# Rounding of the weights by integer steps on three engines, with half of the feature turns moved ahead of the key sums

## The chip, the cores and the metric

The kernel runs on 1 core of one Trainium2 chip. The metric is the device time of one launch in microseconds (us), as the median of 3 runs. All engines of the core work at once: TensorE (PE, matmuls, transposes by matmul; PEld is its weight load), VectorE (DVE), ScalarE (ACT), GpSimd (POOL) and SyncE (SP, which here only issues DMAs). A queue of instructions belongs to each; an engine works its queue in order and waits on semaphores.

## The reference

```python
# polysketch attention, (batch, heads, seq, head_dim) = (4, 4, 1088, 32), r = 8
def phi(x):
    a = np.einsum('rd,bhsd->bhsr', S1, x)
    b = np.einsum('rd,bhsd->bhsr', S2, x)
    return np.einsum('bhsi,bhsj->bhsij', a, b).reshape(*x.shape[:-1], r * r)
q_p, k_p = (phi(q), phi(k))
kv = np.einsum('bhsf,bhsd->bhfd', k_p, v)
z = np.sum(k_p, axis=2)
num = np.einsum('bhsf,bhfd->bhsd', q_p, kv)
den = np.einsum('bhsf,bhf->bhs', q_p, z)[..., None] + 1e-06
attn = (num / den).astype(np.float32)
# bridge to (4352, 128), then a feed-forward block with d_ff = 2048
x = attn.transpose(0, 2, 1, 3).reshape(B * S, H * D)
h = x @ w_in
g = np.where(h > 0.0, h, np.exp(np.minimum(h, 0.0)) - 1.0)
out = (g @ w_out).astype(np.float32)
```

q, k and v are float32. S1, S2, w_in (128 x 2048) and w_out (2048 x 128) come as float64, so the kernel reads each weight as two 32-bit words, a low and a high one, and makes the float32 itself ("rounding" below).

## The kernel before

The schedule is written out by hand: the order of the Python calls is the order in each engine's queue.

**Groups and steps.** The 4352 rows of x are cut into 9 groups g of up to 512 rows, transposed (`xg`, 128 features by 512 rows). The 16 blocks of 128 hidden columns go in 8 pairs cp. A step (g, cp) is `mm1` (two matmuls of xg with W[:, cp], each in column strips by `quarters`, L256, into PSUM tiles h), then `elu`: on ScalarE a relu of -h (L861) and exp (L863) into e, on VectorE max(e - 1, h) into gg (L869); then, two steps later, the second product of that step: `mm2` (L256, o<-gg), `mm2_blocks` (L766) for group 1, or `mm2_seven` (L790) for later groups, which uses a 7-product scheme whose sums `sums7` GpSimd makes (L751 to L754) and whose weight sums SS `weights7` makes on GpSimd (L738). The loop over n at L1108 does mm1 of step n, then the extra work put there with `at`, then elu of the first half, the extra work of `mid`, elu of the second half, the extra work of `late`, then the second product of step n - 2. There are four h banks, so two steps.

**Start of the kernel.** Up to 16 us nothing of the feed-forward block can run: the key features (`KF`, `KO_first`), the key sums (`KA`, L435, into kv), their transpose (`KS_first`, L481 to L483: ScalarE copies kv to kd, TensorE transposes it, ScalarE copies the result to kvS), the query features qp (`q2_den`, `q2_out`, L588 to L609, in two halves), the turn of qp by TensorE transposes (`q4_early`, L621, two halves, each copied to qpT by ScalarE, L622), the product with kvS (`q5_early`, L628, xps) and the copies to xg (L634). `keep_warm` (L264) issues matmuls on constants into a bank nobody reads. The first two steps are written out by hand between L957 and L1000 (`mm1_first`, `elu_a`, `elu_d`), and the sums `KT_out(0)` (L444, a VectorE transpose of kv, with DMAs behind it) come at the end of step 3. kv lies in the PSUM bank ("o1") that `mm2_blocks` takes for group 1.

**The weights.** 16 loads of 256 KB (L174, on SP) fill raw tiles with the two words of each weight; five such tiles, which also serve as tt in `sums7`. Rounding goes in pieces (`order`, L177): pieces 0 to 5 are 256 columns wide (0: w_in of pair 0, 1: w_in of pair 1, 2 and 3: w_out of pairs 0 and 1, 4 and 5: w_in and w_out of pair 2), pieces 6 to 10 are both halves of pairs 3 to 7, 512 columns. One piece takes these passes:

- RA: `round_a` (L102, VectorE): W = high word AND the exponent's mask.
- RB: `round_b` (L107, ScalarE): relu(8 W + bias), the new exponent.
- RC: on VectorE `round_s` (L117, the sign), `round_m` (L121, the mantissa's high bits), `round_d` (L129, low word times 2^-32 plus those) and `round_e` (L137, product of both). For piece 7 the last is two GpSimd passes instead (L134, L135).

For pieces 0 and 1, sign, mantissa and `round_d` are done for both at once (`RC_2`). In the loop, RA stands in `at` of a step, RB in `late` of it, RC in `at` of the next; piece 6 has its RA at step 3, 5 at 4, 7 at 5, 8 at 7, 9 at 9, 10 at 11. In the start, q2_den(0) carries RA(0) between its parts and q2_out carries RA(1) between its halves.

**Other work that stands in the loop** and shares the queues: `transp` (L280, VectorE transposes of k and q), `KF_late_out` (L375), `KO` for batch 1 (L322, GpSimd, 1280 columns), `Z_share` and `make_SWs` (L316, L470, L471, GpSimd), and at step 12 the queries' sums (`queries`, L551 on TensorE; `q1_out_two`, L564, four VectorE transposes, two in `at`, two in `mid`).

Of the kernel before, what the change touches and what calls it, by code (L numbers as in the profile page):

```python
# [17 lines left out]
EXP = mybir.ActivationFunctionType.Exp  # L18
RELU = mybir.ActivationFunctionType.Relu
# [8 lines left out]
def kernel(  # L28
# [21 lines left out]
    nc = tc.nc  # L50
# [44 lines left out]
    tiny = const.tile([P, 1], F32, name="tiny")  # L95
    nc.gpsimd.memset(tiny[:], 2.0 ** -20)

# [14 lines left out]
    def words(raw):  # L112
        return (raw[:, :, 0], raw[:, :, 1]) if len(raw.shape) == 3 else (raw[:, :, :, 0], raw[:, :, :, 1])
# [17 lines left out]
    def round_e(raw, dst, pool=False):  # L131
        mant = words(raw)[0].bitcast(F32)
        if pool:
            nc.gpsimd.tensor_mul(mant, mant, _ap(tiny[:], [[0, dst.shape[1]]]))  # L134
            nc.gpsimd.tensor_mul(dst, mant, dst)  # L135
        else:
            nc.vector.scalar_tensor_tensor(dst, mant, 2.0 ** -20, dst, op0=MUL, op1=MUL)  # L137


    S16 = const.tile([2 * R, D], F32, name="S16")  # L140
# [38 lines left out]
    def round_w(f, i, *a):  # L179
        if wide:  # L180
            cp, w_in, w_out = order[i]
            c = slice(0 if w_in else 2 * P, 4 * P if w_out else 2 * P)
            f(raw_w[cp][:, c], W[:, cp, c], *a)

    def RA(i):
        round_w(round_a, i)

    def RB(i):
        round_w(round_b, i)


    def RC_2():
        if wide:
            for f in (round_s, round_m, round_d):
                f(raw_2[:, :, :2 * P], W[:, :2, :2 * P])

    def RS(i):
        round_w(round_s, i)

    def RM(i):  # L200
        round_w(round_m, i)

    def RD(i):
        round_w(round_d, i)

    def RE(i):
        round_w(round_e, i)

    def RC(i, pool=False):
        round_w(round_c, i)  # L210
        round_w(round_d, i)
        round_w(round_e, i, pool)

    load_v(0)
    load_w(0, 0)
# [260 lines left out]
            z_tile(0, ps, i)  # L476
        return ps, ZC(0, ps)

    def KS_first():
        kd = work.tile([P, 2, R * R], F32, name="kd", tag="kd", bufs=1)  # L480
        nc.scalar.copy(kd[:], _ap(kv_ps[0][:, :R * R], [[0, 2], [1, R * R]]))  # L481
        nc.tensor.transpose(kv_ps[0][:, 128:256], kd[:].rearrange("p w f -> p (w f)"), ident[:])
        nc.scalar.copy(kvS[:].rearrange("p h d -> p (h d)"), kv_ps[0][:, 128:256])  # L483

    NH = B * NT
# [35 lines left out]
    def q1_second():  # L521
        p = psum.tile([P, 512], F32, name="abwp", tag="h", bufs=4)
        for i in range(4):
# [5 lines left out]
        abw[1] = work.tile([P, H * 4, 3 * R], F32, name="abw1", tag="abq1", bufs=1)  # L529
        nc.scalar.copy(abw[1][:].rearrange("p (h t) y -> p h t y", h=H),  # L530
                       p[:, :384].rearrange("p (t h y) -> p h t y", t=4, h=H))
# [80 lines left out]
    def q4_early(g):  # L612

        qpT[g] = work.tile([P, H, 2, P], F32, name="qpT", tag="qpT", bufs=2)
        for hh in range(2):
            p = psum.tile([P, 512], F32, name="qtp", tag="aux")
            for h2 in range(2):
                for m in range(2):
                    o = (h2 * 2 + m) * P
                    r = (2 * hh + h2) * 4 + 2 * m  # L620
                    nc.tensor.transpose(p[:, o:o + P], qp[g][:, r:r + 2].rearrange("p t i j -> p (t i j)"), ident[:])  # L621
            nc.scalar.copy(qpT[g][:, 2 * hh:2 * hh + 2], p[:].rearrange("p (h m s) -> p h m s", h=2, m=2))  # L622

    def q5_early(g):
        xp = [psum.tile([P, 512], F32, name="xps", tag="aux") for _ in range(2)]
        for h in range(H):
            for w in range(2):
                nc.tensor.matmul(xp[w][D * h:D * h + D, :256], kvS[64 * w:64 * w + 64, h, :],  # L628
                                 qpT[g][64 * w:64 * w + 64, h].rearrange("p m s -> p (m s)"),
                                 skip_group_check=True, tile_position=(64 * w, D * h))  # L630
        xg[g] = work.tile([P, 512], F32, name="xg", tag="xg", bufs=3)
        to = xg[g][:].rearrange("p (m w s) -> p w m s", w=2, s=P)
        for w in range(2):
            nc.scalar.copy(to[:, w], xp[w][:, :256].rearrange("p (m s) -> p m s", s=P))  # L634


    exch = [raw_2[:, c].bitcast(F32).rearrange("p (e m a) w -> p e m (a w)", e=2, a=16) if wide else
# [319 lines left out]
    KO_first(7, KT)  # L957
    keep_warm(1, 96, 64)
    zq = q1z_first()
    q2_den(0, zq, lambda: RA(0))  # L960
    q2_out(0, 2, lambda: RA(1))
    KA(0)
    KS_first()
    keep_warm(1)
    RB(0)
    RB(1)
    q4_early(0)
    transp(qT, "q", 0, 8, NT)
    RC_2()
    RE(0)  # L970
    RE(1)
    q1_second()
    q5_early(0)
    keep_warm(1, 192, width[0])
    mm1_first()
    q2(1, 2, lambda: RA(2))
    RB(2)
    elu_a(0, 0, 0)
    elu_a(0, 0, 1, (0,))
    mm1(0, 1, (0,))  # L980
    q4_early(1)
    elu_d(0, 0, 0)
    mm1(0, 1, (1,))
    elu_a(0, 0, 1, (1,))
    RC(2)
    RA(3)
    elu_a(0, 1, 0, (0,))
    RB(3)
    q5_early(1)
    elu_d(0, 0, 1)  # L990
    mm2(0, 0, True, False)
    RA(4)
    for f in (RS, RM, RD):
        f(3)
    elu_a(0, 1, 0, (1,))
    elu_a(0, 1, 1)
    RB(4)
    elu_d(0, 1, 0)
    RE(3)
    elu_d(0, 1, 1)  # L1000


# [8 lines left out]
    def at(n, f, *a):  # L1011
        extra.setdefault(n, []).append((f, *a))
# [4 lines left out]
    def late(n, f, *a):  # L1017
        extra.setdefault((n, 1), []).append((f, *a))

    at(2, RC, 4)  # L1020
    for n, i in ((4, 6), (5, 5), (6, 7), (8, 8), (10, 9), (12, 10)):
        at(n - 1, RA, i)
        late(n - 1, RB, i)
        at(n, RC, i, i == 7)

    late(2, make_Sxp)
    late(3, keep_last, 0)
# [176 lines left out]
```

## Time and profile before

| what | value |
|---|---|
| timed runs | 262.29, 261.77, 261.96 us; median 261.96 |
| the profiled execution | span 260.6 us from the first to the last instruction; no other time is recorded for it; the median lies 1.36 us above the span |
| TensorE clock granted | 0.998 of full speed |
| busy before 16.25 us | PE 14.15, DVE 12.48, ACT 6.69, POOL 7.53 us |
| busy 16.25 to 30.30 (14.05 us) | PE 14.05, DVE 13.11, ACT 12.70, POOL 0 us |
| busy 30.30 to 63.00 (32.70 us) | PE 32.70, DVE 31.83, ACT 23.84, POOL 6.64 us |
| busy 63 to 257 (194 us) | PE 193.87, DVE 129.52, ACT 139.94, POOL 144.78 us |

Lines of the profile are read so: in a list of groups, "L102 DVE TENSOR_SCALAR W<-raw 128x256 uint32<-128x256 uint32 x6 | 1.7, 286 | 0.0" is line 102, its engine and operation, the tile written and the one read, the shapes, the count, total busy us, mean ns of one, and idle us before them. In a timeline or in the chain, the first two numbers are the start and the length in us; in brackets stands the idle time before and what ended it. A span can be of several instructions (x2). Consecutive passes of VectorE overlap by some 0.08 us where they do not depend on each other, those of ScalarE by some 0.10.

### The profile page before, as it was taken

The numbers are of one execution on the slowest core, as the hardware profiler recorded it, in microseconds if no ns is written. First come the engines' busy times: TensorE is split into PE (matmuls) and PEld (weight loads), VectorE is DVE, ScalarE is ACT, GpSimd is POOL, SyncE is SP. The second block draws the span as 40 slices with busy tenths as digits, with TensorE's granted clock in tenths as the row PEclk, the third lists the DMA queues.
The fourth block names the chain that finished last, engine by engine and source line by source line (L and its number), as shares of the span: only waits on it lengthen the run. The fifth ranks groups of instructions, "written<-read, shape, count | busy, mean of one in ns | idle before, by whom it ended". The sixth has DMA issues, their size and how long they took to land.

```text
span 260.6 us, 9756 instructions
## 1 busy us (share of the span) xinstructions
PE 254.8 (98%) x4123; PEld 158.4 (61%) x4123; DVE 186.9 (72%) x352; ACT 183.4 (70%) x358; POOL 159.0 (61%) x202
## 2 busy tenths in 40 slices
PE   8899999999999999999999999999999999999994
PEld 6753333453346667666666666665666666668993
DVE  6799999999988967997477675744466746544651
ACT  2379968766667577776687777775877777777792
POOL 3520007002179996788678798888688888887310
PEclk9999999999999999999999999999999999999999
DMA  5998079012112210002100204220001110110021
GB/s 173 330 358 222 3 223 268 24 21 85 28 18 28 31 34 18 3 15 34 20 0 4 33 10 104 60 30 13 3 3 27 34 26 3 25 19 3 3 30 33
DMA packets 30379, 15.61 MB, mean 60 GB/s; under 512 B 22496, under 2 KB 28000, under 8 KB 30336
## 3 DMA queue, kind: packets, MB, share of 16 engines
q1 hardware_dynamic: 29904, 14.63, 23.0%
q8 instruction: 32, 0.52, 0.9%
q10 hardware_dynamic: 368, 0.30, 0.3%
q0 software_dynamic: 64, 0.07, 0.1%
q14 instruction: 11, 0.09, 0.1%
HBM read 11.31 MB, written 2.36 MB: 52 GB/s over the span
## 4 chain that ended last, share of the span: by engine, by line
PE 97%; DVE 1%; ACT 0%; issue 0%; DVEq 0%
PE h L256 45%; PE pb L790 17%; PE pa L790 13%; PE o L256 5%; PE pb L766 4%; PE ol L256 3%; PE idle L264 1%; PE kv L435 1%; PE abp L343 1%; PE h L681 1%; PE h L551 1%; PE qtp L621 1%; DVE qp L609 1%; PE h L693 1%; PE xps L628 0%; PE kfps L365 0%
## 5 line engine op out<-in xcount | busy, mean ns | idle before, releaser
L256 PE MATMUL h<-xg,W 128*32 128x512 f32 (+3 forms) x904 | 130.8, 539 | 0.4 <-ACT xg L634 0.4
L869 DVE SCALAR_TENSOR_TENSOR gg<-e,h 128x512 f32<-128x512 f32 x128 | 85.9, 681 | 52.6 <-ACT e L863 47.8
L861 ACT ACTIVATE e<-h 128x512 f32<-128x512 f32 x128 | 75.5, 590 | 46.2 <-PE h L256 46.0
L863 ACT ACTIVATE e<-e 128x512 f32<-128x512 f32 x128 | 80.9, 632 | 3.8
L751 POOL TENSOR_TENSOR tt<-gg 128x512 f32<-128x512 f32 x50 | 64.3, 1286 | 28.9 <-DVE gg L869 25.2
L256 PEld LDWEIGHTS h<-xg,W 128*32 128x32 f32 (+1 forms) x904 | 43.0, 122 | 43.0 <-issue 34.4
L754 POOL TENSOR_TENSOR tt<-gg,tt 128x256 f32<-128x256 f32 x50 | 36.9, 739 | 3.9
L753 POOL TENSOR_TENSOR tt<-tt,gg 128x256 f32<-128x256 f32 x50 | 36.7, 734 | 3.9
L790 PEld LDWEIGHTS pa<-gg,W 128*64 128x64 f32 (+1 forms) x496 | 23.7, 126 | 22.4 <-issue 22.2
L790 PE MATMUL pa<-gg,W 128*64 128x128 f32 (+1 forms) x496 | 30.6, 274 | 0.0
L790 PE MATMUL pb<-tt,SS 128*64 128x128 f32 (+1 forms) x480 | 29.6, 273 | 0.0
L790 PEld LDWEIGHTS pb<-tt,SS 128*64 128x64 f32 (+1 forms) x480 | 22.8, 126 | 0.0
L790 PE MATMUL pa<-tt,SS 128*32 128x128 f32 (+1 forms) x288 | 21.2, 273 | 0.0
L790 PE MATMUL pb<-gg,SS 128*64 128x128 f32 (+1 forms) x256 | 19.9, 273 | 0.0
L790 PE MATMUL pb<-tt,W 128*64 128x128 f32 (+1 forms) x256 | 19.9, 273 | 0.0
L134 POOL TENSOR_TENSOR raw<-raw,tiny 128x512 f32<-128x512 f32 x1 | 1.0, 1041 | 24.7 <-DVE raw L129 24.7
L256 PE MATMUL o<-gg,W 128*32 128x512 f32 x128 | 15.3, 595 | 0.0
L790 PEld LDWEIGHTS pa<-tt,SS 128*32 128x32 f32 (+1 forms) x288 | 13.7, 124 | 0.0
L790 PEld LDWEIGHTS pb<-gg,SS 128*64 128x64 f32 (+1 forms) x256 | 12.8, 125 | 0.0
L790 PEld LDWEIGHTS pb<-tt,W 128*64 128x64 f32 (+1 forms) x256 | 12.8, 125 | 0.0
L766 PE MATMUL pb<-gg,W 128*32 128x256 f32 x192 | 11.5, 380 | 0.0
L921 DVE SCALAR_TENSOR_TENSOR gg<-e,h 128x256 f32<-128x256 f32 x16 | 6.6, 418 | 6.4 <-PE h L256 3.2
(163 smaller groups left out, 269.3 us busy)
## 6 DMA issues: line engine op xcount, KB each, us to landing
raw<-in_moe_w_in_dram SPq DMA_DIRECT2D x8, 256.0 KB, 6.3
raw<-in_moe_w_out_dram SPq DMA_DIRECT2D x8, 256.0 KB, 6.5
out_dram<-ob SPq DMA_DIRECT2D x112, 16.0 KB, 1.5
hd_k<-in_k_dram SPq DMA_DIRECT2D x3, 544.0 KB, 7.5
hd_q<-in_q_dram SPq DMA_DIRECT2D x3, 544.0 KB, 8.5
v<-in_v_dram SPq DMA_DIRECT2D x4, 288.0 KB, 7.1
v<-in_v_dram SPq DMA_DIRECT2D x4, 256.0 KB, 8.4
raw<-qpF SPq DMA_DIRECT2D x16, 64.0 KB, 2.0
```

The source lines that it names most:

```text
L256: nc.tensor.matmul(dst[c:c + tile], lhs[:, c:c + tile], rhs, skip_group_check=True, tile_position=(0, c), **kw)
L264: nc.tensor.matmul(idle[c:c + tile, :cols], ones[:, :tile], ones[:, :cols], skip_group_check=True, tile_position=(0, c))
L343: nc.tensor.matmul(ps[i // 5][64 * u:64 * u + 64, 64 * (i % 5):64 * (i % 5) + 64], kT[b][:, u * KT + i, :], Sab[:].rearrange("p h y -> p ( ...
L751: nc.gpsimd.tensor_tensor(_ap(t[:, 0], [[4 * P, 2], [P, 2], [1, P]]), _ap(gs[g, cp][:, 0, P:], [[4 * P, 2]] + us), _ap(gs[g, cp][:, 0], [[ ...
L753: nc.gpsimd.tensor_tensor(t[:, 1], t[:, 2], b11, op=ADD)
L754: nc.gpsimd.tensor_tensor(t[:, 3], b21, t[:, 1], op=SUB)
L766: nc.tensor.matmul(acc[1][0][r:r + width[0], 256 * hi:256 * hi + 256], lhs[:, w:w + width[0]], gg[:, c, 256 * u:256 * u + 256], start=(cp ...
L790: nc.tensor.matmul(bank[r:r + width[0], P * col:P * col + P], lhs[:, w:w + width[0]], rhs[:, u], start=(first and i in ((0,) if g == 1 els ...
L861: nc.scalar.activation(e, hs[g, cp][c][:, :n], RELU, scale=-1.0)
L863: nc.scalar.activation(e, e, EXP, scale=-1.0)
L869: nc.vector.scalar_tensor_tensor(gs[g, cp][:, c, :n], es[g, cp][:, c, :n], -1.0, hs[g, cp][c][:, :n], op0=ADD, op1=MAX)
L921: nc.vector.scalar_tensor_tensor(gs["last", k // 2][:, k % 2, :2 * P], es["last", k // 2][:, k % 2, :2 * P], -1.0, hs["last", k][:, :2 * P ...
```

## The change

Rounding now takes these passes for a piece, where lo and hi are the two words:

- strip: W = hi without the sign bit, on VectorE (an AND) or, for pieces 0 to 3, on ScalarE (Abs).
- floor: W = max(W, 2^-15) on VectorE; shift: W = W << 3 on VectorE.
- low: lo = 2^-51 lo + 2 on ScalarE (Identity), so that its bits are the rounded top bits of the low word.
- whole: W = W + lo as integers on GpSimd.
- `round_s`: the sign, on VectorE, as before.

So RA is strip, floor and shift; RB is low and whole; RC is `round_s` alone. `round_m` and `round_d` stay only for S1 and S2, `round_e` and `RC_2` are gone. In the loop RC moves from `at` to `mid`, behind the elu of the first half; `mid` entries stand in the order in which they are registered, so at step 12 it comes behind the first two `q1_out_two` transposes and ahead of the other two. The weight sums of the last two pairs move from `at` to `late` of step 12.

In the start, the first half of the turns of qp is issued on TensorE ahead of the transpose of the key sums, which was ahead of both; `KS_first` is cut into its ScalarE copy and the rest. VectorE copies half of the second qpT and one of the two xg halves of group 0. The second group's features (`q1_second`) are made in two parts, the second behind `q5_early`; the last `keep_warm` is 64 columns and not 192. On TensorE the order is now: key sums, keep_warm, four turns, the sums' transpose, four turns, half of q1_second, xps, the other half, keep_warm, the first h. In GpSimd's queue the whole passes of pieces 0 to 4 come ahead of make_Sxp and make_SWs, on ScalarE's strip(0), low(0) and strip(1) come ahead of kd, and low(1) between kvS and qpT.

```diff
+    def strip(raw, dst, eng=nc.vector):
+        if eng is nc.vector:
+            nc.vector.tensor_scalar(dst.bitcast(U32), words(raw)[1], 0x7FFFFFFF, None, op0=AND)
+        else:
+            nc.scalar.activation(dst, words(raw)[1].bitcast(F32), ABS)
+
+    def floor(raw, dst):
+        nc.vector.tensor_scalar_max(dst, dst, 2.0 ** -15)
+
+    def shift(raw, dst):
+        nc.vector.tensor_scalar(dst.bitcast(U32), dst.bitcast(U32), 3, None, op0=SHL)
+
+    def low(raw, dst):
+        lo = words(raw)[0]
+        nc.scalar.activation(lo.bitcast(F32), lo, IDENTITY, scale=2.0 ** -51, bias=two[:dst.shape[0]])
+
+    def whole(raw, dst):
+        nc.gpsimd.tensor_tensor(dst.bitcast(U32), dst.bitcast(U32), words(raw)[0], op=ADD)
...
     def RA(i):
-        round_w(round_a, i)
+        for f in (strip, floor, shift):
+            R1(f, i)
     def RB(i):
-        round_w(round_b, i)
+        R1(low, i)
+        R1(whole, i)
-    def RC(i, pool=False):
-        round_w(round_c, i)
-        round_w(round_d, i)
-        round_w(round_e, i, pool)
+    def RC(i):
+        R1(round_s, i)
...
+    def q4_out(g, hh, p, split=False):
+        if split:
+            nc.vector.tensor_copy(qpT[g][:, 2 * hh + 1], p[:, 2 * P:].rearrange("p (m s) -> p m s", m=2))
+            nc.scalar.copy(qpT[g][:, 2 * hh], p[:, :2 * P].rearrange("p (m s) -> p m s", m=2))
+        else:
             nc.scalar.copy(qpT[g][:, 2 * hh:2 * hh + 2], p[:].rearrange("p (h m s) -> p h m s", h=2, m=2))
...
         for w in range(2):
-            nc.scalar.copy(to[:, w], xp[w][:, :256].rearrange("p (m s) -> p m s", s=P))
+            (nc.vector.tensor_copy if split and w else nc.scalar.copy)(
+                to[:, w], xp[w][:, :256].rearrange("p (m s) -> p m s", s=P))
...
-    q2_den(0, zq, lambda: RA(0))
-    q2_out(0, 2, lambda: RA(1))
+    R1(strip, 0, nc.scalar)
+    R1(floor, 0)
+    R1(low, 0)
+    q2_den(0, zq)
+    q2_out(0, 2)
     KA(0)
-    KS_first()
     keep_warm(1)
-    RB(0)
-    RB(1)
-    q4_early(0)
+    R1(strip, 1, nc.scalar)
+    KS_first_a()
+    qpT_a = q4_early(0, (0,))
+    KS_first_b()
+    R1(low, 1)
+    R1(shift, 0)
+    R1(whole, 0)
     transp(qT, "q", 0, 8, NT)
-    RC_2()
-    RE(0)
-    RE(1)
-    q1_second()
-    q5_early(0)
-    keep_warm(1, 192, width[0])
+    q4_out(0, 0, qpT_a)
+    q4_out(0, 1, q4_early(0, (1,)), True)
+    R1(round_s, 0)
+    R1(floor, 1)
+    R1(shift, 1)
+    R1(whole, 1)
+    q1_second((0, 1))
+    R1(strip, 2, nc.scalar)
+    R1(low, 2)
+    q5_early(0, True)
+    R1(round_s, 1)
+    q1_second((2, 3))
+    keep_warm(1, 64, width[0])
     mm1_first()
-    q2(1, 2, lambda: RA(2))
-    RB(2)
+    q2(1, 2, lambda: R1(floor, 2))
+    R1(shift, 2)
+    R1(whole, 2)
     elu_a(0, 0, 0)
+    R1(strip, 3, nc.scalar)
     elu_a(0, 0, 1, (0,))
...
-    RC(2)
-    RA(3)
+    R1(low, 3)
+    R1(floor, 3)
+    R1(shift, 3)
+    R1(whole, 3)
+    R1(round_s, 2)
     elu_a(0, 1, 0, (0,))
-    RB(3)
...
     RA(4)
-    for f in (RS, RM, RD):
-        f(3)
     elu_a(0, 1, 0, (1,))
     elu_a(0, 1, 1)
+    R1(round_s, 3)
     RB(4)
     elu_d(0, 1, 0)
-    RE(3)
     elu_d(0, 1, 1)
...
-    at(2, RC, 4)
+    mid(2, RC, 4)
     for n, i in ((4, 6), (5, 5), (6, 7), (8, 8), (10, 9), (12, 10)):
         at(n - 1, RA, i)
         late(n - 1, RB, i)
-        at(n, RC, i, i == 7)
+        mid(n, RC, i)
...
         if nx == 2:
-            at(n, weights7, slice(NP - 2, NP))
+            late(n, weights7, slice(NP - 2, NP))
             at(n, q1_out_two, (0, 1))
             mid(n, q1_out_two, (2, 3))
```

More of the change, by code (lines that the diff above doesn't have):

```diff
@@ L18 @@
 EXP = mybir.ActivationFunctionType.Exp
+IDENTITY = mybir.ActivationFunctionType.Identity
+ABS = mybir.ActivationFunctionType.Abs
 RELU = mybir.ActivationFunctionType.Relu
@@ L94 @@
     nc.vector.memset(ebias[:], -float(896 << 23))
-    tiny = const.tile([P, 1], F32, name="tiny")
-    nc.gpsimd.memset(tiny[:], 2.0 ** -20)
+    two = const.tile([P, 1], F32, name="two")
+    nc.gpsimd.memset(two[:], 2.0)
     def round_a(raw, dst):
@@ L129, in round_d @@
         nc.vector.scalar_tensor_tensor(lo.bitcast(F32), lo, 2.0 ** -32, hi, op0=MUL, op1=ADD)
[L131 to L137, printed above, removed]
     S16 = const.tile([2 * R, D], F32, name="S16")
@@ L183, in round_w @@
             f(raw_w[cp][:, c], W[:, cp, c], *a)
+    R1 = round_w
     def RA(i):
-        round_w(round_a, i)
+        for f in (strip, floor, shift):
+            R1(f, i)
     def RB(i):
-        round_w(round_b, i)
[L192 to L203, printed above, removed]
-        round_w(round_d, i)
-    def RE(i):
-        round_w(round_e, i)
-    def RC(i, pool=False):
-        round_w(round_c, i)
-        round_w(round_d, i)
-        round_w(round_e, i, pool)
+        R1(low, i)
+        R1(whole, i)
+    def RC(i):
+        R1(round_s, i)
     load_v(0)
@@ L477, in Z_first, with KS_first_a, KS_first_b @@
         return ps, ZC(0, ps)
-    def KS_first():
-        kd = work.tile([P, 2, R * R], F32, name="kd", tag="kd", bufs=1)
+    def KS_first_a():
+        kd = feats["kd"] = work.tile([P, 2, R * R], F32, name="kd", tag="kd", bufs=1)
         nc.scalar.copy(kd[:], _ap(kv_ps[0][:, :R * R], [[0, 2], [1, R * R]]))
-        nc.tensor.transpose(kv_ps[0][:, 128:256], kd[:].rearrange("p w f -> p (w f)"), ident[:])
+    def KS_first_b():
+        nc.tensor.transpose(kv_ps[0][:, 128:256], feats.pop("kd")[:].rearrange("p w f -> p (w f)"), ident[:])
         nc.scalar.copy(kvS[:].rearrange("p h d -> p (h d)"), kv_ps[0][:, 128:256])
@@ L519, in q1z_first, with q1_second @@
         return p[:, :128].rearrange("p (t h r) -> p h t r", t=4, h=H)
-    def q1_second():
-        p = psum.tile([P, 512], F32, name="abwp", tag="h", bufs=4)
-        for i in range(4):
+    def q1_second(tiles):
+        if 1 not in abw:
+            abw[1, 0] = psum.tile([P, 512], F32, name="abwp", tag="h", bufs=4)
+            abw[1] = work.tile([P, H * 4, 3 * R], F32, name="abw1", tag="abq1", bufs=1)
+        p = abw[1, 0]
+        for i in tiles:
             for u in range(2):
@@ L528, in q1_second @@
                                  tile_position=(0, 64 * u))
-        abw[1] = work.tile([P, H * 4, 3 * R], F32, name="abw1", tag="abq1", bufs=1)
-        nc.scalar.copy(abw[1][:].rearrange("p (h t) y -> p h t y", h=H),
-                       p[:, :384].rearrange("p (t h y) -> p h t y", t=4, h=H))
+        if 3 in tiles:
+            nc.scalar.copy(abw[1][:].rearrange("p (h t) y -> p h t y", h=H),
+                           p[:, :384].rearrange("p (t h y) -> p h t y", t=4, h=H))
     units = {g: ([g, g + 1] if 4 <= g < NQ - 1 else [g]) for g in [2, 3] + list(range(4, NQ, 2))}
@@ L610, in q2_out, with q4_early @@
                                  _ap(b_, [b_.ap[1], [0, R], b_.ap[2]]))
-    def q4_early(g):
-        qpT[g] = work.tile([P, H, 2, P], F32, name="qpT", tag="qpT", bufs=2)
-        for hh in range(2):
+    def q4_early(g, halves=(0, 1)):
+        if 0 in halves:
+            qpT[g] = work.tile([P, H, 2, P], F32, name="qpT", tag="qpT", bufs=2)
+        for hh in halves:
             p = psum.tile([P, 512], F32, name="qtp", tag="aux")
@@ L621, in q4_early, with q5_early @@
                     nc.tensor.transpose(p[:, o:o + P], qp[g][:, r:r + 2].rearrange("p t i j -> p (t i j)"), ident[:])
+            if len(halves) == 1:
+                return p
+            q4_out(g, hh, p)
+    def q4_out(g, hh, p, split=False):
[3 more added lines that the diff above has]
+        else:
             nc.scalar.copy(qpT[g][:, 2 * hh:2 * hh + 2], p[:].rearrange("p (h m s) -> p h m s", h=2, m=2))
-    def q5_early(g):
+    def q5_early(g, split=False):
         xp = [psum.tile([P, 512], F32, name="xps", tag="aux") for _ in range(2)]
```

## The prediction

> **What bounds the kernel now.** I read the page first (part 1, busy time), then the chain in order of time, then the timelines of VectorE, GpSimd and TensorE where that chain leaves TensorE or starts a new group.
>
> ```profile
> PE 254.8 (98%) x4123; PEld 158.4 (61%) x4123; DVE 186.9 (72%) x352; ACT 183.4 (70%) x358; POOL 159.0 (61%) x202
> ```
>
> TensorE is busy for 98% of the 260.6 us span, and the other engines have room on average. So no pass that is merely shorter pays anything. What pays or costs is the moment at which TensorE gets an operand. The chain says where it ever waits:
>
> ```profile
> 14.81 0.70 PE xps L628 x16
> 15.52 0.64 ACT xg L634 x2
> 16.25 2.79 PE h L256 x40
> 19.04 1.02 PE qtp L621 x8
> 20.07 0.99 PE h L256 x8
> ```
>
> The last step that is not TensorE's is the pair of xg copies; after 16.25 us the groups follow each other to the end. So a delay of TensorE after 16.25 stays to the end, and a gain counts only if every later operand comes earlier too. Three places have hardly any room. The first is L766 (mm2_blocks, which takes over the PSUM bank that KT_out frees), VectorE then TensorE:
>
> ```profile
> 27.81 0.44 DVE L102 TENSOR_SCALAR W<-raw 128x512 uint32<-128x512 uint32 x1
> 28.25 0.69 DVE L869 SCALAR_TENSOR_TENSOR gg<-e,h 128x512 f32<-128x512 f32 x1
> 29.39 0.69 DVE L869 SCALAR_TENSOR_TENSOR gg<-e,h 128x512 f32<-128x512 f32 x1 [0.45 <-ACT e L863]
> 30.00 0.24 DVE L444 STREAM_TRANSPOSE kvt<-kv 128x64 f32<-128x64 f32 x1
> ```
>
> ```profile
> 30.29 1.07 PE L766 MATMUL pb<-gg,W 128*32 128x256 f32 x16
> ```
>
> L444 ends at 30.24 and L766 starts at 30.29: no slack. The second is mm2(0, 2), which needs weight piece 5; the third is mm1 of step 13, which needs piece 10:
>
> ```profile
> 61.48 0.77 DVE L564 STREAM_TRANSPOSE abw<-h 128x256 f32<-128x256 f32 x2
> 62.17 0.65 DVE L869 SCALAR_TENSOR_TENSOR gg<-e,h 128x512 f32<-128x512 f32 x1
> ```
>
> ```profile
> 62.39 1.91 PE L256 MATMUL h<-xg,W 128*32 128x512 f32 x16
> ```
>
> Before, piece 10 was done (L137, 60.85 to 61.56) ahead of these two VectorE rows, 0.8 us early.
>
> **Prices of the new passes.** No row shows them, so by neighbours. strip, floor and shift on VectorE: L102 at 256 columns 0.29 us, at 512 0.44; ends 0.25 (L594, 128x16, nearly all of it fixed cost) and 0.42/0.69 (the two-input L117); I take L102, the same kind of instruction, and 0.03 for each dependence (L593 to L594: 11.05 to 11.08). round_s: L117, 0.42 and 0.69. strip and low on ScalarE: between 0.42 (L916, 128x256) and 0.51 (L107, 128x256, integers); I take 0.50, and for 512 L107's 0.71. whole on GpSimd: between 1.04 (L134) and 2.62 (L322, its longest) at 512 columns; I take L135's 1.31, which reads the same stride-2 words; at 256 columns L753's 0.74. VectorE's copy from PSUM, 128x256: 0.27 to 0.42, 0.40 taken. It runs beside ScalarE's copy of 0.37.
>
> **Part 1, up to the first h (16.25).** strip(0) moves to ScalarE into its idle stretch after 9.53; the trace's landing event of this weight piece is at 9.43, so it runs 9.55 to 10.05 and floor(0) is through VectorE before pw can start (10.34, by zqp). Cover: if the transfer landed at 10.5, floor(0), ahead of pw, would cost up to 0.5. strip(1) waits for a landing at 10.94, ends at 11.45, and kd (11.43 before) starts 0.02 to 0.05 late: nothing, since its transpose now stands behind the first four turns of qp, which wait for the qp half that ends at 12.38. RA(1) no longer sits between the qp halves: the second ends at 13.0 and not 13.19. The turns end near 13.75 instead of 13.96. But ScalarE now has kvS (behind the moved transpose, 13.25), low(1) 0.50, qpT 0.59 and half of the other qpT 0.37 in a row, and ends at 14.7 where it ended at 14.59. VectorE's half of that copy is done by then. So xps starts about as before (14.74). The xg halves, 0.65 in a row before, now run side by side in 0.40: done at 15.8 instead of 16.15. W of piece 0: shift 13.2, whole 13.3 to 14.1, round_s to 14.6, no longer the 16.10 of L137. The first h starts near 15.9: a gain of 0.35. The smaller keep_warm is in a gap and worth nothing.
>
> **Part 2, 16 to 30.3.** ScalarE runs almost without a pause from 17.81 (the first L861) to 30. It starts 0.35 earlier, but strip(3) is added between L863 and L861 (0.50 less the 0.10 by which two L107 overlap: 0.91 for both); low(3) and low(4) replace L107 one for one. So the e tiles come when they came. On VectorE RA(6) becomes three passes where L102 was one, ahead of both gg of step 3: from 27.8 it ends at 29.2 instead of 28.24, the two gg end at 29.8 and 30.4 instead of 28.94 and 30.08, and L444 at 30.5 instead of 30.24. With what is left of the earlier start I take +0.1 at L766 (ends -0.35, nothing lost, and +0.3). The 0.35 is gone here.
>
> **Part 3, the second place (37.96).** GpSimd now holds a weight pass of 1.31 while VectorE works. What that does, the trace shows at 42 us, VectorE and GpSimd:
>
> ```profile
> 42.19 0.96 DVE L102 TENSOR_SCALAR W<-raw 128x512 uint32<-128x512 uint32 x1
> 43.06 1.29 DVE L869 SCALAR_TENSOR_TENSOR gg<-e,h 128x512 f32<-128x512 f32 x2
> 44.26 1.72 DVE L117 SCALAR_TENSOR_TENSOR W<-raw,W 128x512 uint32<-128x512 uint32 x1
> ```
>
> ```profile
> 41.54 1.31 POOL L135 TENSOR_TENSOR W<-raw,W 128x512 f32<-128x512 f32 x1
> 42.81 2.62 POOL L322 TENSOR_TENSOR kp<-abk 128x1280 f32<-128x1280 f32 x1
> ```
>
> L102 took 0.96 instead of 0.44 and ended after L135; L117 took 1.72 instead of 0.69 and ended 0.55 after L322. gg, with one operand in PSUM, ran its usual 0.69. So VectorE's weight passes wait for a running GpSimd pass. whole(6) runs 30.0 to 31.3 behind low(6) (29.27 to 29.98, where L107 stood). strip(5) is ready at 30.5 and ends at 31.5; floor and shift at 32.2; the kT transpose (1.34) at 33.5; gg, round_s(6), gg at 35.3; RA(7) at 36.7; gg at 37.3. whole(7) starts at 36.8, when shift(7) ends, and holds until 38.1. round_s(5) stands behind that gg and ends at 38.5, and mm2(0, 2), at 38.06 by then, waits: +0.4. Ends: 0 if the passes go side by side (round_s(5) then ends before 37), +0.9 if whole is 0.4 longer. Behind the waiting round_s stand gg of step 5 and what follows, with two steps of room.
>
> The Trainium skill, page "SBUF — State Buffer", section "Who interferes with whom", says that VectorE's two-port passes and those with two SBUF inputs share one port pair with GpSimd, whoever starts first holding it for its whole instruction. By it, too, the sum has its +0.4, without it 0; the 1.72 us row agrees.
>
> **Part 4, the third place (62.39).** RC(10) moves from before the L564 transposes to behind gg of step 12, and is round_s alone (0.69). The queries' sums leave TensorE at about 60.85 (their last matmul starts at 60.33). Two transposes start at 60.9 and 61.25, gg at 61.6, round_s at 62.2, and it ends at 62.9. mm1 of step 13 starts at 62.95 instead of 62.39: +0.5 (ends +0.4 and +0.65).
>
> **What costs nothing.** weights7 a little later: its tiles are read first at L790, 76.8, 13 us after L738. Sxp and SWs behind five whole passes on GpSimd: they end near 26.5 and are read at 37.3. The last weight load and the k, v, q loads behind it on SP start at 32.8 when a raw buffer comes free; that is now round_s(6), 34.7: they land by 50 and are read after 56. KO on GpSimd (2.62) delays floor(8) by that much, and gg of step 7 by 2; its h bank is asked for two steps (6.9 us) later.
>
> **The sum.** +0.1 +0.4 +0.5 = +1.0 on a span of 260.6, so 261.6. The median run is 261.96, 1.36 above the span; I keep that: 263.0.
>
> **Rivals.** (A) GpSimd and VectorE pass each other: part 3 is 0, the sum +0.6, 262.55. For it: the contended rows are few. Against: both are whole passes late. (B) Not slower: the contiguous floor and shift are faster than the strided L102 (0.25), so RA(6) ends by 28.8, VectorE has L444 done when TensorE asks, and the lead of 0.35 outlives L766; part 3 falls to 0 as RA(7) and round_s(5) end ahead of whole(7). It decides at L766: a start below 30.0. -0.35 +0.5 gives +0.15, 262.1; with round_s(10) in time too, 261.6. Against it: L121, the same on its own words, also takes 0.30 and 0.43. (C) The integer add is dearer than the float passes: 2.6 at 512 columns. round_s(1), in VectorE's queue ahead of pw, then makes the second turns 0.6 late (+0.4 left at L766), and whole(7) ends 1.3 later: +0.4 +1.7 +0.5, 264.6. Nothing in the trace speaks for it but that no integer row of GpSimd exists.
>
> **Chances.** Forecast 0.55, A 0.15, B 0.16, C 0.14. A measurement of this kernel tells about 0.2% (0.52 us) from no change: faster is below 261.44, slower above 262.48. Faster: half of B, 0.08. Within: the rest of B and two thirds of A, 0.18. Slower: 0.74. The range runs from 261.9 (most of B out) to 264.2 (most of C out).
>
> **What would show it.** Right: h first near 15.9; L444's successor and TensorE at 30.3 to 30.5; a TensorE gap before mm2(0, 2), ended by a round_s that lies under a GpSimd pass; one before mm1 of step 13, ended by round_s(10). Wrong: whole far from 1.31 or 0.74, no gap at 38 with passes overlapping at full speed, or TensorE still 0.3 ahead at L766.

## The result

The changed kernel takes 262.93 us (median of 5 executions, 262.71 to 263.24); the kernel before, timed beside it, 262.05 (median of 5, 261.77 to 262.29). The ratio is 1.0034, 95% interval 1.0021 to 1.0046: slower by 0.9 us, with a time close to the forecast (263.0). The profiled execution has a span of 261.2 us and a time of 262.96. All line numbers from here on are those of the changed kernel, where not said otherwise.

The first part of its page shows the work moved as described, and TensorE no less in demand:

```profile
PE 254.4 (97%) x4123; PEld 157.4 (60%) x4123; DVE 182.8 (70%) x343; ACT 184.4 (71%) x361; POOL 166.7 (64%) x211
```

Cut at five starts that both profiles have, the spans compare so (us):

| stretch | before | changed | difference |
|---|---|---|---|
| start to pw of group 0 (VectorE, first query features) | 10.34 | 10.35 | +0.01 |
| pw to the first h (TensorE) | 5.91 | 5.59 | -0.32 |
| first h to L779, which is L766 before | 14.04 | 14.36 | +0.32 |
| L779 to the first mm2 of piece 5 | 7.67 | 7.80 | +0.13 |
| that to mm1 of step 13 | 24.43 | 24.88 | +0.45 |
| that to the end | 198.21 | 198.22 | +0.01 |

Behind mm1 of step 13 nothing changed. The first h comes 0.32 earlier, and three places behind it cost 0.32, 0.13 and 0.45; counted from pw, mm1 of step 13 starts 0.59 later. Pieces of the chain of the changed kernel, in order of time:

```profile
3.96 5.67 DMA raw<-in_moe_w_in_dram
11.68 1.29 DVE qp L611 x2
...
16.12 1.34 PE h L254 x24
17.48 0.61 ACT e L874
...
28.81 1.28 DVE gg L882 x2
30.25 1.17 DVE W L127
...
36.84 1.22 DVE W L119
38.10 1.92 PE o L254 x16
...
61.00 0.76 DVE abw L566 x2
62.98 1.92 PE h L254 x16
```

The chain of before held nothing but TensorE's groups from 16.25 on. Now it leaves TensorE at 17.48 and goes through ScalarE and VectorE without a break as far as 38.10, with gg, the strip (L127) and the sign (L119) of piece 5 in it; it leaves TensorE once more at 61.00, for the transposes of step 12 (L566), gg and the sign of piece 10. At its head stands a weight load.

**First place.** VectorE's timeline ahead of L779 (start, length, line, operation, tiles):

```profile
27.54 0.43 DVE L127 TENSOR_SCALAR W<-raw 128x512 uint32<-128x512 uint32 x1
28.00 0.43 DVE L132 TENSOR_SCALAR W<-W 128x512 f32<-128x512 f32 x1
28.46 0.43 DVE L135 TENSOR_SCALAR W<-W 128x512 uint32<-128x512 uint32 x1
28.81 1.28 DVE L882 SCALAR_TENSOR_TENSOR gg<-e,h 128x512 f32<-128x512 f32 x2
30.00 0.24 DVE L442 STREAM_TRANSPOSE kvt<-kv 128x64 f32<-128x64 f32 x1
30.17 1.24 DVE L127 TENSOR_SCALAR W<-raw 128x256 uint32<-128x256 uint32 x1
```

Three passes of piece 6 stand where one stood. No bracket marks idle time: both gg and L442 end when VectorE gets to them, at the same 30.24 as before, and L779 starts at 30.30 instead of 30.29. The mm1 ahead of L779 starts at 28.26, that is 17.91 behind pw, where before had 18.13. From there to L779 TensorE takes 1.82 in the kernel before and 2.04 here. So 0.22 of the lead of 0.32 is lost at L779; the other 0.10 was lost at the turns of the next group, near 19.8 us.

**Second place.** TensorE's mm2 of piece 5 in the kernel before, then GpSimd's whole passes of pieces 6 and 7 and VectorE's sign pass of piece 5 in the changed one:

```profile
37.96 1.92 PE L256 MATMUL o<-gg,W 128*32 128x512 f32 x16
```

```profile
29.95 1.30 POOL L142 TENSOR_TENSOR W<-W,raw 128x512 uint32<-128x512 uint32 x1 [3.47 <-ACT raw L139]
...
36.46 1.30 POOL L142 TENSOR_TENSOR W<-W,raw 128x512 uint32<-128x512 uint32 x1 [3.03 <-DVE W L135]
```

```profile
36.84 1.20 DVE L119 SCALAR_TENSOR_TENSOR W<-raw,W 128x256 uint32<-128x256 uint32 x1
```

L119 at 256 columns takes 0.42 elsewhere and 1.20 here; it ends at 38.04, 0.28 after whole(7). TensorE's mm2 follows at 38.10, 0.13 later behind pw than before. The strip of piece 5 in the fence before (1.24 instead of 0.29) ends 0.15 after whole(6) in the same way.

**Third place.** The sign pass of piece 10 on VectorE, and TensorE behind it:

```profile
62.26 0.67 DVE L119 SCALAR_TENSOR_TENSOR W<-raw,W 128x512 uint32<-128x512 uint32 x1
```

```profile
62.98 1.49 PE L254 MATMUL h<-xg,W 128*32 128x512 f32 x12 [0.27 <-DVE W L119]
```

**The head** holds what the table hides. ScalarE's and VectorE's timelines, then TensorE's:

```profile
9.65 0.45 ACT L129 ACTIVATE W<-raw 128x256 f32<-128x256 f32 x1 [0.64 <-DMA raw<-in_moe_w_in_dram]
```

```profile
10.14 0.29 DVE L132 TENSOR_SCALAR W<-W 128x256 f32<-128x256 f32 x1 [0.55 <-ACT W L129]
10.35 0.28 DVE L590 TENSOR_TENSOR pw<-abq,zqp 128x128 f32<-128x128 f32 x1
```

```profile
9.05 0.66 PE L517 MATMUL zqp<-SW,qT 128*64 128x32 f32 x16 [0.17 <-DVE SW L463]
```

zqp, the operand of pw, is done at 9.70. VectorE has waited 0.55 for strip(0), and with it for a weight load, because floor(0) stands ahead of pw in its queue. Before, zqp was done at 10.22 in the profile and pw started at once. Both profiles have pw at 10.35, for different reasons.

### The profile page after: what moved, and what is told of

It is laid out like the page before. It is cut to its first block, busy times and chain, and to the rows that moved or that the text cites. A ratio compares the mean times of both kernels' runs of the same rounds, so it can differ in the third digit from the quotient of the medians.

```text
span 261.2 us, 9782 instructions
## 1 busy us (share of the span) xinstructions
PE 254.4 (97%) x4123; PEld 157.4 (60%) x4123; DVE 182.8 (70%) x343; ACT 184.4 (71%) x361; POOL 166.7 (64%) x211
## 4 chain that ended last, share of the span: by engine, by line
PE 85%; DVE 6%; ACT 3%; DMA 2%; issue 1%; SPq 1%; DVEq 0%
PE h L254 41%; PE pb L803 17%; PE pa L803 13%; PE o L254 3%; PE ol L254 3%; PE pb L779 3%; DMA raw<-in_moe_w_in_dram 2%; DVE gg L882 2%; PE kv L433 1%; DVE W L127 1%; DVE W L119 1%; ACT e L876 1%; PE h L694 1%; ACT e L874 1%; DVE W L132 1%
## 5 line engine op out<-in xcount | busy, mean ns | idle before, releaser
L766 POOL TENSOR_TENSOR tt<-tt,gg 128x256 f32<-128x256 f32 x50 | 36.8, 737 | 3.9
L142 POOL TENSOR_TENSOR W<-W,raw 128x256 uint32<-128x256 uint32 (+1 forms) x11 | 11.0, 999 | 26.7 <-ACT raw L139 14.2
L779 PE MATMUL pb<-gg,W 128*32 128x256 f32 x192 | 11.5, 380 | 0.1
```

What stands on the lines that cost most here:

```text
L142: nc.gpsimd.tensor_tensor(dst.bitcast(U32), dst.bitcast(U32), words(raw)[0], op=ADD)
L766: nc.gpsimd.tensor_tensor(t[:, 1], t[:, 2], b11, op=ADD)
L779: nc.tensor.matmul(acc[1][0][r:r + width[0], 256 * hi:256 * hi + 256], lhs[:, w:w + width[0]], gg[:, c, 256 * u:256 * u + 256], start=(cp ...
```

## The experiments

Each run is given with its median and its ratio to the kernel before, timed in the same comparison. The times of one kernel spread by 0.3 to 1.6 us. In the profiles, executions of one order differ ahead of pw and hardly behind it, so the places are read from the profiles and counted from the start of pw (us; zqp and pw themselves from the start of the span):

| run | zqp done | pw | first h | L779 | mm2, piece 5 | mm1, step 13 | end |
|---|---|---|---|---|---|---|---|
| before | 10.22 | 10.34 | 5.91 | 19.95 | 27.62 | 52.05 | 250.23 |
| before, again (e9) | 10.14 | 10.26 | 5.92 | 19.95 | 27.62 | 52.05 | 250.26 |
| changed | 9.70 | 10.35 | 5.59 | 19.95 | 27.75 | 52.64 | 250.84 |
| e1 piece 10 early | 9.61 | 10.02 | 5.59 | 19.93 | 27.79 | 52.22 | 250.41 |
| e2 piece 5 early | 10.15 | 10.19 | 5.59 | 19.96 | 27.63 | 52.53 | 250.73 |
| e3 (same order as changed) | 10.03 | 10.20 | 5.59 | 19.98 | 27.79 | 52.68 | 250.88 |
| e4 head undone | 9.61 | 10.19 | 5.29 | 19.79 | 27.59 | 52.48 | 250.70 |
| e5 piece 6 in the gap | 9.62 | 10.15 | 5.58 | 19.76 | 27.60 | 52.50 | 250.73 |
| e6 floor behind pw | 9.71 | 9.82 | 5.65 | 19.99 | 27.82 | 52.71 | 250.92 |
| e10 the same again | 9.69 | 9.80 | 5.60 | 19.95 | 27.81 | 52.70 | 250.90 |
| e7 kd first | 10.10 | 10.31 | 5.53 | 19.88 | 27.72 | 52.61 | 250.82 |
| e8 all places | 10.00 | 10.12 | 5.30 | 19.61 | 27.28 | 51.71 | 249.92 |
| e11 all places, floor ahead | 9.77 | 10.45 | 5.29 | 19.59 | 27.25 | 51.68 | 249.87 |
| e12 all places, xg shared | 9.74 | 9.86 | 5.30 | 19.61 | 27.28 | 51.70 | 249.89 |

Rows of the same order (the first two; changed and e3; e6 and e10) agree within 0.05 in every column behind pw, so differences of 0.1 count here.

**e1: the sign pass of piece 10 ahead of the transposes of step 12.**

```diff
-        mid(n, RC, i)
+        (at if i == 10 else mid)(n, RC, i)
```

> The sign pass of piece 10 goes ahead of the two L566 transposes of step 12 instead of behind gg; nothing else changes. In the changed kernel whole(10) ends at 60.37, VectorE stands idle from 59.02 to 60.98, and mm1 of step 13 starts at 62.98 after the sign pass of 62.26 to 62.93. Theory (the place of this pass is what holds step 13): the pass runs near 60.4 to 61.1, the transposes start 0.1 later, and mm1 of step 13 starts near 62.55, which is before's 62.39 plus the 0.14 already lost at 38; the time falls by 0.43 to 262.5. Rival 1 (the transposes free a bank that mm1 needs, and 0.1 later is too late for it): only 0.2 comes back, 262.7. Rival 2 (step 13 is late for another reason, the pass only happens to end there): no change, 262.9.

Measured: 262.70 (11 executions), ratio 1.0027 (1.0018 to 1.0035). VectorE's and TensorE's timelines:

```profile
60.11 0.74 DVE L119 SCALAR_TENSOR_TENSOR W<-raw,W 128x512 uint32<-128x512 uint32 x1 [1.37 <-POOL W L142]
```

```profile
62.24 1.48 PE L254 MATMUL h<-xg,W 128*32 128x512 f32 x12
```

The pass now fills idle time, TensorE has no gap (no bracket), and mm1 of step 13 stands 52.22 behind pw instead of 52.64: the 0.43 is back to the end (250.41). The theory holds in the steps; the median of the times moved by 0.23 only, as these executions spread from 262.24 to 263.22.

**e2: the sign pass of piece 5 ahead of piece 7's passes.** The same edit with `i == 5`.

> The sign pass of piece 5 goes ahead of strip, floor and shift of piece 7 in step 5, where whole(5) has been done since 33.43 and GpSimd runs no pass. In the changed kernel the pass took 1.20 us (36.84 to 38.04) under whole(7) (36.46 to 37.76), and the first mm2 of piece 5 started at 38.10. Theory (VectorE's two-input pass waits for the GpSimd pass that runs): it takes 0.42 near 35.0 to 35.5, strip(7) to shift(7) and whole(7) come 0.3 to 0.4 later, and TensorE has no gap at 38: 37.96 instead of 38.10; the stall at step 13 is unchanged in size, so mm1 of step 13 starts near 62.84 and the time falls by 0.14 to 262.8. Rival (VectorE is simply full here, and the same work in another order ends as late): the gap moves to the next mm2 or mm1 within two steps and the time stays at 262.9.

Measured: 262.78, ratio 1.0034 (1.0021 to 1.0046). VectorE, GpSimd, TensorE:

```profile
34.84 0.42 DVE L119 SCALAR_TENSOR_TENSOR W<-raw,W 128x256 uint32<-128x256 uint32 x1
```

```profile
36.66 1.30 POOL L142 TENSOR_TENSOR W<-W,raw 128x512 uint32<-128x512 uint32 x1 [3.37 <-DVE W L135]
```

```profile
37.83 1.07 PE L254 MATMUL o<-gg,W 128*32 128x512 f32 x8
```

Away from a GpSimd pass it takes 0.42, mm2 stands 27.63 behind pw, as before, and 0.11 is kept to the end. The theory holds; the rival is out, as no gap came in its place.

**e3 and e5: piece 6 away from the gg of step 3.** e3 used `late(2, ...)` for strip and floor, e5 `at(2, ...)`:

```diff
-        at(n - 1, RA, i)
+        if i == 6:
+            at(2, R1, strip, 6)
+            at(2, R1, floor, 6)
+            at(3, R1, shift, 6)
+        else:
+            at(n - 1, RA, i)
```

> strip and floor of piece 6 go to the end of step 2 and its shift stays at the head of step 3, so that one pass instead of three stands ahead of the two gg of step 3. In the changed kernel the three ran 27.54 to 28.89, gg 28.81 to 30.09, the STREAM_TRANSPOSE L442 at 30.00, and TensorE's L779 at 30.30 with a gap of 0.14. Theory (the three VectorE passes hold L779 and eat the lead of the first h): the two passes fill the idle stretch after 24.90, the second gg starts when its e is there (29.20), L442 starts near 29.83, and L779 at 30.16, where TensorE is free; 0.14 is gained and kept: 262.8. Rival (ScalarE's e tiles set this place, as they did in the kernel before): L779 stays within 0.05 of 30.30 and the time at 262.9.

e3 missed its aim: nothing stands on VectorE between the end of step 2 and the head of step 3, so no queue changed. It is the changed kernel once more: 262.94, ratio 1.0038 (1.0025 to 1.0052).

> The run before it of piece 6 put strip and floor at the end of step 2, where VectorE has nothing between them and the head of step 3, so VectorE's order stayed as it was. Here they go to the head of step 2, ahead of its first gg, into an idle stretch of 0.9 us (24.90 to 25.78 in the changed kernel); shift stays at the head of step 3. Counted from the start of pw, since the head varies from run to run: in the changed kernel the first h starts 5.59 after pw and L779 19.95 after pw. Theory (three VectorE passes ahead of the two gg hold L779): L779 starts 19.80 after pw, where TensorE is free; 0.15 is gained: 262.8. Rival (ScalarE's e tiles or TensorE itself set the place): L779 stays at 19.95 and the time at 262.9.

Measured: 262.77, ratio 1.0029 (1.0018 to 1.0040). VectorE, GpSimd, TensorE:

```profile
24.61 0.91 DVE L127 TENSOR_SCALAR W<-raw 128x512 uint32<-128x512 uint32 x1
...
29.62 0.24 DVE L442 STREAM_TRANSPOSE kvt<-kv 128x64 f32<-128x64 f32 x1
29.78 0.25 DVE L127 TENSOR_SCALAR W<-raw 128x256 uint32<-128x256 uint32 x1
30.07 1.29 DVE L132 TENSOR_SCALAR W<-W 128x256 f32<-128x256 f32 x1
```

```profile
29.74 1.46 POOL L142 TENSOR_TENSOR W<-W,raw 128x512 uint32<-128x512 uint32 x1 [3.15 <-ACT raw L139]
```

```profile
29.92 0.85 PE L779 MATMUL pb<-gg,W 128*32 128x256 f32 x12
```

L442 and L779 come 0.19 earlier behind pw (19.76) though the strip itself took 0.91, beside the whole pass of piece 4. So in the changed kernel the three VectorE passes held L779, not ScalarE. With them gone the second gg waits for ScalarE's e (0.46 us), which is the next limit. Of the 0.19, 0.14 is left at step 13 (52.50) and 0.11 at the end (250.73).

**e4 and e7: the head.** e4 turns all of it back; e7 puts only the order back and leaves the copies shared:

```diff
-    qpT_a = q4_early(0, (0,))
     KS_first_b()
     R1(low, 1)
+    qpT_a = q4_early(0, (0,))
```

> The changed rounding and its order stay, but the head is turned back: all eight turns of qp stand behind the transpose of kd, ScalarE alone copies qpT and both xg halves. Theory (the head's gain is 0.3 at the first h and is lost at L779, which VectorE's passes hold): the first h starts 0.3 later than in the changed kernel (near 16.2 to 16.3), L779 at 30.30 to 30.45, and the time is 262.9 to 263.1: the head's change is worth 0 to 0.15. Rival 1 (the gain is carried to the end): 263.25. Rival 2 (the head's change is worth nothing even at the first h, because the last weight piece or the ScalarE queue holds it): first h at 15.95, time 262.9.

Measured: 262.75, ratio 1.0033 (1.0020 to 1.0045). The first h stands 5.29 behind pw, not 5.59: the head's change costs 0.3 there, which no theory had, and 0.14 at the end. ScalarE's timeline of e4, then of the changed kernel:

```profile
12.15 0.54 ACT L139 ACTIVATE raw<-raw,two 128x256 f32<-128x256 uint32 x1
12.96 1.25 ACT L634 COPY qpT<-qtp 128x512 f32<-128x512 f32 x2 [0.27 <-PE qtp L624]
14.11 0.44 ACT L129 ACTIVATE W<-raw 128x256 f32<-128x256 f32 x1
14.45 0.53 ACT L139 ACTIVATE raw<-raw,two 128x256 f32<-128x256 uint32 x1
15.00 0.65 ACT L646 COPY xg<-xps 128x256 f32<-128x256 f32 x2
```

```profile
13.39 0.54 ACT L139 ACTIVATE raw<-raw,two 128x256 f32<-128x256 uint32 x1
13.82 0.59 ACT L634 COPY qpT<-qtp 128x512 f32<-128x512 f32 x1
14.29 0.40 ACT L632 COPY qpT<-qtp 128x256 f32<-128x256 f32 x1
...
15.47 0.37 ACT L646 COPY xg<-xps 128x256 f32<-128x256 f32 x1
```

With kd's transpose behind the first turns, kvS and low(1) come 1.24 later (1.08 counted from pw) and stand ahead of the qpT copies in ScalarE's queue. The last of these copies ends at 14.21 in e4 and at 14.68 in the changed kernel. TensorE's xps, which reads qpT, in e4 and in the changed kernel:

```profile
14.24 0.68 PE L640 MATMUL xps<-qpT,kvS 64*32 64x256 f32 x16
```

```profile
14.46 0.93 PE L640 MATMUL xps<-qpT,kvS 64*32 64x256 f32 x16
```

The half of q1_second ahead of xps starts 3.57 behind pw in both, when the transpose of qT is done. In e4 xps then runs through; in the changed kernel it has to wait for the copies and ends 5.04 behind pw instead of 4.73. This is the 0.3 at the first h.

> kd's transpose, kvS and low(1) go back ahead of the turns of qp; the copies stay shared between ScalarE and VectorE. With the whole head turned back the first h started 5.28 after pw and not 5.59. Theory (the half-turn costs: kvS comes 1.2 later and pushes low(1), 0.54, in front of the qpT copies on ScalarE; VectorE's copies gain): the first h starts 5.05 to 5.25 after pw, L779 19.70 to 19.80 after pw instead of 19.95, the time falls by 0.15 to 0.25, to 262.75. Rival 1 (VectorE's copies cost and the half-turn does not): 5.59 stays, 262.93. Rival 2 (the first turns of q1_second, which wait for the qT transposes, hold xps in either order): 5.28 as with the old head, and the copies are worth nothing.

Measured: 262.91, ratio 1.0033 (1.0020 to 1.0046); first h 5.53 behind pw. The theory fails: the order alone is worth 0.06, because the shared copy then takes its place. ScalarE and VectorE of e7:

```profile
14.21 0.37 ACT L632 COPY qpT<-qtp 128x256 f32<-128x256 f32 x1 [0.54 <-DVE qpT L631]
```

```profile
13.75 0.42 DVE L631 COPY qpT<-qtp 128x256 f32<-128x256 f32 x1
```

VectorE's half has to wait for the 0.77 transpose of qT ahead of it, and ScalarE's half of the same tile waits for VectorE's: the two do not run side by side, and the last copy ends at 14.58, 0.25 later behind pw than in e4. xps takes 0.93 again. In the changed kernel the late low(1) covers this wait (L632 has no bracket there); the new order with an unshared copy was not tried.

**e6 and e10: floor(0) between pw and den.**

```diff
-    R1(floor, 0)
     R1(low, 0)
-    q2_den(0, zq)
+    q2_den(0, zq, lambda: R1(floor, 0))
```

> floor(0) goes behind pw on VectorE, between pw and den, where RA(0) stood in the kernel before; nothing else changes. In the five profiles of the changed order floor(0) waits for strip(0), which starts when its weight piece lands (9.35 to 9.65), and pw starts 0.21 behind floor, though zqp was done 0.0 to 0.55 earlier (0.28 in the mean). Theory (the wait for the weight's landing, ahead of pw, costs this head 0.28 in the mean, and that is the part of the slowdown that the steps do not explain): pw starts 0.1 behind the end of zqp, den no more than 0.15 later behind it than before, and the time falls by 0.2 to 0.3, to 262.65. Rival (floor(0) behind pw still waits for the same landing and holds den): pw is early but den is not, 262.9.

> The run with floor(0) between pw and den once more: its five executions had spans of 260.7 to 261.4, wider than those of the changed kernel (260.9 to 261.4). Theory (floor(0) ahead of pw costs the changed kernel's head 0.3 to 0.4; the three later executions of the first look had a late head): the median of these five lies at 262.6 to 262.75. Rival (with the turned head something else waits for the same landings, so that floor's place is worth nothing): 262.9 again.

Measured: 262.97 (5 executions), ratio 1.0032 (1.0020 to 1.0045), then 262.53 (7), ratio 1.0025 (1.0015 to 1.0036). VectorE of the second:

```profile
9.80 0.29 DVE L590 TENSOR_TENSOR pw<-abq,zqp 128x128 f32<-128x128 f32 x1 [0.23 <-PE zqp L517]
10.01 0.29 DVE L132 TENSOR_SCALAR W<-W 128x256 f32<-128x256 f32 x1
10.21 0.30 DVE L595 TENSOR_REDUCE den<-pw 128x16 f32<-128x144 f32 x1
```

pw waits for zqp alone and starts 0.55 earlier than in the profile of the changed kernel, where zqp was done at the same time; den follows 0.41 behind, with floor between, against 0.38 without. The twelve times, from two comparisons, have a median of 262.6 and a mean of 262.74; the ten of the changed order (with e3, also from two) have 262.94 for both. The five executions of e6 alone, three of them late, would have told against it.

**e8, e11, e12: all places at once.** e8 is the changed rounding with the edits of e1, e2, e5, e6 and the head of e4; e11 has floor(0) ahead of pw; e12 is e8 with the xg copies shared (`q5_early(0, True)`).

> The changed rounding with every place mended: the head turned back, floor(0) between pw and den, strip and floor of piece 6 at the head of step 2, the sign passes of pieces 5 and 10 at the heads of steps 5 and 12. Theory: against the changed kernel -0.28 (pw), -0.3 (first h to L779, nothing held there), -0.12 (38 us), -0.43 (63 us), -1.1 in all: 261.8, that is 0.1 to 0.2 below the kernel before (261.9 to 262.05). Rival (VectorE is as full as before and one of the later weight passes, of pieces 7 to 9, becomes late in its place): 262.1 to 262.4.

> The kernel with all places mended, but floor(0) ahead of pw as in the changed kernel. Theory (the place of floor(0) costs the head 0.3 to 0.4): 262.0 against 261.67 with floor behind pw, pw 0.7 behind the start of strip(0). Rival (the place is worth nothing): 261.65 to 261.75.

> The kernel with all places mended, the old order in the head, and one thing of the change's head kept: VectorE copies the second half of xg beside ScalarE. With all places mended the xg halves ran 14.95 to 15.59 on ScalarE and the first h started 5.30 after pw, L779 19.61 after pw with no gap ahead of it. Theory (this copy is the part of the head's change that gains): first h 5.00 to 5.10 after pw, L779 19.35 to 19.45, time 261.4 to 261.5, below the kernel before by 0.4. Rival (L442 ended only 0.05 before L779, and ScalarE's chain of e tiles from the first L874 to 29 us does not move with the first h): L779 stays at 19.60 and the time at 261.65.

Measured: e8 261.67 (11 executions), ratio 0.9992 (0.9983 to 1.0001); e11 262.14 (11), ratio 1.0009 (1.0000 to 1.0017), spans with a median of 260.2 against 259.8 in e8: floor's place is worth 0.4, as expected. The two come from separate comparisons, in which the kernel before took 261.91 and 261.90. The chain of e8 around the second place is TensorE alone again:

```profile
35.10 1.72 PE h L254 x16
36.82 0.65 PE kfps L363 x16
37.46 1.85 PE o L254 x16
```

From pw to the end e8 takes 249.92, 0.92 less than the changed kernel and 0.3 less than before. e12: 261.73 (11), ratio 0.9990 (0.9981 to 0.9998), and no difference to e8 in any column: TensorE goes from the second half of q1_second through keep_warm into the first h, and the half of xg that the first h reads is copied by then. The rival's figures for L779 and the time came out, but neither of the two had the first h unmoved.

**e9: the kernel before, again.** 

> The kernel before, unchanged, for a second profile of it. Its 17 timed executions of the last comparison have spans of 260.0 to 260.5 (median 260.1) for times of 261.76 to 262.32 (median 261.91), so 1.75 to 1.8 lies around the span; the profile that the forecast started from has 260.6 and pw at 10.34. Theory (that profile was a late execution: its head, not its steps, was 0.45 behind the usual one): the usual execution has pw 0.1 behind the end of zqp and ahead of the changed kernel's, near 9.85 to 9.95, while first h, L766, the first mm2 of piece 5 and mm1 of step 13 stand 5.91, 19.95, 27.62 and 52.05 behind pw as in the first profile. Rival (the head is the same in all executions and something in the steps differs): pw at 10.3 again and other distances.

Measured: 262.26 (12 executions, 261.83 to 263.42), while the same kernel took 261.90 (31 executions) as the one compared with: ratio 1.0013 (1.0001 to 1.0025) between two equal kernels. The distances behind pw are those of the first profile, so the steps are fixed and the head is what varies. By its span (260.5, against a median of 260.1 in the 31) this profile was a late execution too (pw 10.26, time 262.29), so that the usual head of before was not seen; that pw starts near 9.85 in it is worked out, from spans of 260.1 less 250.25. A gain of 0.1% as in e8 and e12 is thus shown by the steps (0.3 us), and hardly by the times.

What makes zqp late stands in the profiles. In all 14, zqp is done 2.45 to 2.47 behind the end of TensorE's 36 matmuls for the key features (abp), which lies between 7.15 and 7.76. Those matmuls in e1, then in e9:

```profile
5.31 1.85 PE L341 MATMUL abp<-Sab,kT 128*64 128x64 f32 x36
```

```profile
5.30 2.38 PE L343 MATMUL abp<-Sab,kT 128*64 128x64 f32 x36
```

They start alike, and the trace lists only one wait of 0.2 us for them in either; but the median matmul takes 222 ns in e1 and 302 in e9, while the granted clock reads 1.00 in both. So it was TensorE's pace that made zqp late here, and not a load. Why the pace differs stays open. strip(0) does wait for a load, and moves independently of this.

## Why the prediction was right, and where it was not

The time came out (263.0 forecast, 262.93 measured), and the three places and their causes were the ones named. That it came out so closely is in part luck: the steps add 0.4 less than forecast, and the time added around the span was about 0.4 too small.

- **Part 1, first h 15.9, gain 0.35.** Measured 15.94 and 0.32. The reason was half wrong. e4, with the new rounding, the cut q1_second and the old order, has 5.29 against 5.91: these are worth 0.62, and the rest of the new head gives 0.30 of it back. It was not taken apart, but the rows show two things that move with it. TensorE's xps ends 4.73 behind pw instead of 5.06: the second half of qp is done 0.24 earlier, and only half of q1_second stands ahead of xps. And W of piece 0 is done at 14.35 in e4, where before had 16.10 (L137), only 0.15 ahead of its first h. In e4 the first h starts at 15.47 while the second xg copy runs until 15.65, so it needs only the first half of xg; before had that half at 15.87 and still started at 16.25. So W, rather than the xg copies, probably held it there. The forecast rightly let ScalarE end at 14.7 with kvS, low(1) and the copies in a row, and xps end as before (5.04 behind pw, 5.06 before); but it did not see that with the old head the first h would have come 0.3 earlier still (e4), and credited 0.25 to the shared xg copies, which were worth nothing where they were tried alone (e12).
- **Part 1, floor(0) ahead of pw, nothing.** This step failed. It read "is through VectorE before pw can start (10.34, by zqp)". zqp's 10.22 was that of one execution, late by its span; zqp is done at 9.6 to 9.8 in more than half of the profiles, while strip(0) starts at 9.35 to 9.76. The cover was named, with its price of up to 0.5, but not how much it varies. By e8 against e11 it is 0.4.
- **Part 2, +0.1 at L779.** Measured 0.0 (19.95 and 19.95 behind pw). The mechanism is shown by e5, and the lead was gone here, as forecast. The passes ran 27.54 to 28.89 instead of 27.8 to 29.2: VectorE started them with the lead it still had.
- **Part 3, +0.4.** Mechanism right, size off: +0.13. shift(7) ended at 36.33 and whole(7) at 37.76, where 36.8 and 38.1 were forecast; the wait in 1.20 us of L119 is as described. e2 takes it away whole.
- **Part 4, +0.5.** Measured +0.45, and e1 gives 0.43 back.
- **The sum and the time around the span.** The steps add +0.59, not +1.0. The 1.36 added for the time around the span set the span of one execution beside the median of others. In every execution that has both, 1.73 to 1.89 lies around the span, but for seven of e8 and e11 (2.20 to 2.39); so the profiled execution before took about 262.3, and 260.6 + 0.6 + 1.75 gives 262.95. Against the usual execution before (span 260.1), the difference of 0.9 to 1.0 is 0.59 from the steps; the rest, 0.3 to 0.4, fits what the place of floor(0) was worth in e11 against e8.
- **The rivals.** A (passes go side by side) falls by the rows of L119 and L127, though its 0 at the second place was nearer to the size than 0.4. B would have shown L779 below 30.0; it stood at 30.30. C falls with whole at 1.30 and 0.74. The other prices held: strip, floor and shift 0.29 and 0.43; Abs 0.43 to 0.47 (0.50 forecast); low 0.54 and 0.78 (0.50 and 0.71).

## What to carry to other kernels

A pass that became cheaper on average still has to be placed: here three short passes ahead of a deadline, one pass behind the wrong neighbour and one ahead of the first link of the chain made a rounding with fewer VectorE passes slower, and moving these (e8) turned it into a slight gain. Before costing an edit at nothing because something else is late, ask whether that lateness is the same in every execution: one profile can hide a wait of 0.4 us behind an operand that happened to come late. Count places from an event behind the varying part, and set a span only beside the time of the same execution.

## What the runs showed of the hardware

- VectorE's weight passes and GpSimd's passes take turns, and the one that starts first goes through. In the changed kernel whole(6) was first and strip(5) took 1.24 instead of 0.29. In e5 the strip of piece 6 had begun at 24.61 when GpSimd's L308 started at 25.18, and L308 took 0.46 instead of 0.24. Also in e5, whole(6) and strip(5) have starts only 0.04 apart (29.74 and 29.78): strip(5) ran its 0.25, whole(6) took 1.46 instead of 1.30, and the floor behind took 1.29. Two gg, which read PSUM, took 1.28 together under whole(7) in e2 (36.44 to 37.72), no more than elsewhere. The Trainium skill, page "SBUF — State Buffer", section "Who interferes with whom", says: "Issue order, not op shape, decides who blocks." Both orders agree with it here.
- An independent pass put between two dependent ones on VectorE is almost free: den starts 0.41 behind pw with a pass of 0.29 between them (e10) and 0.38 without (changed kernel).
- The head of one program moves between executions at unchanged distances behind it. In five profiles with the same head (changed, e1, e2, e3, e5) pw started at 10.02 to 10.35 and the first h 5.59 behind it in each, within 0.01. This is as much as most of the effects here.
